# A fused attention and expert kernel: later weight splits and routing in the first slot, memory pools split in two, five accumulator banks instead of three

## The chip, the core and the metric

The kernel runs on one core of a Trainium2 chip. The metric is the device time of one execution in microseconds. The core has a matrix engine (TensorE, PE), a vector engine (VectorE, DVE), a scalar engine (ScalarE, ACT), a general engine (GpSimd, POOL) and a queue for transfers (SyncE, SP). Each works through its own list of instructions strictly in order; they meet at semaphores. Matmul results go to an accumulator memory (PSUM) of eight banks.

## What is computed

Eight batches of 448 tokens, twelve heads of 64. Attention uses a sigmoid instead of a softmax; its output rows (3584 tokens of 768 numbers) go through a mixture of eight experts, of which each token visits the one with the largest logit:

```python
scores = scale * np.matmul(q, k.transpose(0, 1, 3, 2)) - np.log(S)
attn = 1.0 / (1.0 + np.exp(-scores))
x = np.matmul(attn, v)                      # then (B*S, H*D)
logits = x @ w_gate
e_idx = np.argmax(logits, axis=1)           # one expert a token
for e in range(E):
    mask = e_idx == e
    h = np.maximum(x[mask] @ w1[e], 0.0)
    ye = h @ w2[e]
    out[mask] = gate_w[mask, None] * eom[mask, e, None] * ye
```

## The kernel before

**Attention.** 168 units, each of four score matmuls, a sigmoid on ScalarE and four value matmuls. VectorE adds the two halves of an output, transposes it into `xt` (two buffers, one a batch), and at the end of a batch SyncE stores `xt` to `x_dram`. Every two groups the gate matmuls run; after a batch its *routing* follows, a generator with five pieces (`route`): the logits (TensorE transposes, VectorE reductions), the counts (sigmoids, eight small matmuls), the *places* (ScalarE copies the counts out of PSUM, L257; VectorE takes a reciprocal, L258; some fifteen small GpSimd instructions from L259 to L222 make each token's place in the list of its expert), the *rows* (VectorE's reciprocal L271 of what GpSimd made in L267, GpSimd's L273, then four indirect writes into the list `lst` in DRAM, L275, each waiting for the one ahead).

**Slots.** The experts work in slots of 256 rows of one expert. A slot has layer 1 (eight blocks `f` of 18 matmuls, 6 parts of the 768 inputs by 3 products) and layer 2 (four outputs `i` of 24 matmuls). Numbers are kept as a high part, rounded to the matmul's format, and a low part, the rest; high by high, high by low and low by high are summed. So every operand is *split* in two steps (`split`, L421 and L422): ScalarE casts to the high part, VectorE subtracts to get the low part. For a block, ScalarE's relu (L465) writes the high part of `h` and VectorE (L466) the low part; the block's bank is free after that. Three slots (0 to 2) take rows of the first six batches, and can start before the lists are complete; slots 3 to 13 and two half slots at the end follow in the profiled execution.

**What a slot does for the next one.** In `slot`, SyncE loads the next w1 and, later, w2 (each only where the expert changes), GpSimd gathers the next rows from `x_dram` (L399, eight indirect transfers), VectorE transposes them behind block 7 (`turn_x`, L440), and between the outputs of layer 2 the rows and the three pairs of w1 rows are split. The w2 of the slot itself is split during its layer 1, one quarter (`split_w2(k)`, two of the eight inner parts) behind blocks 0, 2, 4 and 6. ScalarE writes each output `y` out of PSUM (L481), and after two of them GpSimd scatters 128 rows to `out` (L483).

**The order around the change.** Nothing reorders: `manual_schedule` keeps the order in which the code is written. The last batch's routing and the tables and lists of the late slots run beside the first slots as a generator `side()`, of which `slot` takes one step after each of blocks 0 to 6 and after outputs 1, 2 and 3, ten steps a slot. Its pieces are: logits at step 2, counts at step 5, places at step 6, rows at step 7; the late table (`table(True)`, five steps on VectorE, L294 to L363) from step 9; then for five groups of lists SyncE's loads (`load_list`) and, three steps later, a VectorE transpose and twelve GpSimd copies (`spread_lists`, L383 to L390).

**Memory and banks.** The attention's buffers form one pool, freed as a whole; the pool of the slots (`late`: `h`, `y`, `w2h`, `w2l` and others) takes its place, so its first writer waits for every reader of the attention's buffers, the store of the last `xt` among them. `take` hands out PSUM banks in turn from a list: layer 1 takes from `psh`, banks 0, 1, 2, 4, 5, of which `build` keeps the first three once attention is recorded (`self.psh = self.psh[0:3]`); layer 2 takes from `psy`, banks 4, 5, 3. A bank is written again only when its last reader is done. Block 0 of slot 0 is already computed inside the attention (`begun`).

Of the kernel before, what the change touches and what calls it, by code (L numbers as in the profile page):

```python
# [9 lines left out]
F32 = mybir.dt.float32  # L10
F32R = mybir.dt.float32r
# [9 lines left out]
B, H, S, D = 8, 12, 448, 64  # L21
NPAIR = H // 2
E = 8
DM = H * D
# [27 lines left out]
class Kernel:  # L52
# [45 lines left out]
        self.tmp_early = o + 4096  # L98

    def late_memory(self):  # L100
        p = self.pool("late")
        self.hs = [p.tile([128, 8, TS], F32R, name=f"h{i}") for i in range(2)]
        self.ys = [p.tile([128, DM], F32, name=f"y{i}") for i in range(2)]
        hb = p.tile([128, DF], F32, name="hb")
        self.hb = hb
        self.hx = p.tile([128, 4, Q4], F32, name="hx")
        self.w2h = p.tile([128, 8, DM], F32R, name="w2h")
        self.w2l = [p.tile([128, 4, DM], F32R, name=f"w2l{i}") for i in range(2)]
        self.lr = [hb[0:32, 192 * i:192 * i + 192] for i in range(5)]

    def tmp(self, shape, dt=F32):
# [375 lines left out]
    def slot(self, cur, nxt, side=None, begun=False, drain=False):  # L487
        nx = self.load_slot(*nxt) if nxt is not None else None
        if drain:
            self.nc.gpsimd.drain()  # L490
        for f in range(8):
            self.layer1(f, begun and f == 0)
            if f % 2 == 0:
                self.split_w2(f // 2)
            if side is not None and f < 7:
                next(side, None)
        self.load_w2(nx)
        self.turn_x(nx)
        self.split_x(nx, 0)
        self.split_x(nx, 1)  # L500
        for i, (t, n) in enumerate(((0, 0), (0, 1), (1, 0), (1, 1))):
            self.layer2(cur, t, n, self.ys[t])
            if i == 0:
                self.split_x(nx, 2)
            if i < 3 and nx is not None:
                self.split_w1(i)
            if side is not None and i > 0:
                next(side, None)
        return nx
# [57 lines left out]
        if nx is not None:  # L567
            self.split_w1_row(5)

    def attention(self, pool):  # L570
        nc = self.nc
        N = B * NPAIR
        NG = N // G
# [1 line left out]
        t = lambda n, shape: pool.tile(shape, F32, name=n)  # L575
# [4 lines left out]
        at = [t(f"a{i}", [128, 2, S]) for i in range(4)]  # L580
        xts = [t(f"x{i}", [128, S]) for i in range(4)]
        xh = t("xh", [128, S])
        xt = [t(f"xt{i}", [128, S // 32, NPAIR * 32]) for i in range(2)]
        half = [slice(0, 64), slice(64, 128)]
        corners = [(0, 0), (1, 0), (0, 1), (1, 1)]

# [78 lines left out]
        for u in range(U * NG + LAG):  # L665
            g, i = divmod(u, U)
# [52 lines left out]
    def build(self, phases="abc"):  # L719
        tc, nc = self.tc, self.nc  # L720
        ms = tc.manual_schedule()
        ms.__enter__()
        self.constants()
        self.memory()
        with tc.tile_pool(name="attn", bufs=1) as p:
            rt = self.attention(p)
        self.late_memory()
        if phases == "ab":
            for _ in rt:
                pass  # L730
            ms.__exit__(None, None, None)
            return

        early = lambda k: (self.tab_e, k, self.lts[:, k], self.lxs[:, k], ROWS_E)
        late = lambda k: (self.tab_l, k, self.lts[:, EARLY + k], self.lxs[:, EARLY + k])

        def side():
            yield
            next(rt)
            yield  # L740
            yield
            yield
            next(rt)
            yield
            for _ in rt:
                yield
            yield
            for _ in self.table(True):
                yield
            nc.gpsimd.memset(self.lr[3], 0.0)  # L750
            groups = [(a, min(a + 4, LATE_N)) for a in range(0, LATE_N, 4)]

            def load(i):
                if i < len(groups):
                    a, b = groups[i]
                    for k in range(a, b):
                        self.load_list(self.tab_l, k, self.lr[i][8 * (k - a):8 * (k - a) + 8], 8)
                else:
                    for k in range(E):
                        self.load_list(self.tab_b, k, self.lr[i][4 * k:4 * k + 4], 4)  # L760

            def spread(i):
                if i < len(groups):
                    a, b = (EARLY + k for k in groups[i])
                    self.spread_lists(self.lr[i], self.lts[:, a:b], self.lxs[:, a:b])
                else:
                    self.spread_lists(self.lr[i], self.ltb, self.lxb)

            for i in range(len(groups) + 1):
                load(i)  # L770
                for _ in range(3):
                    yield
                spread(i)

        self.psh = self.psh[0:3]
        sd = side()
        self.mm_ps = self.mm_late
        cur = self.s0
        for k in range(EARLY - 1):
            cur = self.slot(cur, early(k + 1), sd, k == 0)  # L780
        cur = self.slot(cur, late(0), sd)
        for k in range(LATE_MIN):
            if k == LATE_MIN - 1:
                full = nc.values_load(self.tot[0:1, 0:1], min_val=0, max_val=LATE_MAX)
                part = nc.values_load(self.tot[0:1, 1:2], min_val=0, max_val=E)
                self.gather(dict(lx=self.lxb[:, 1], xg=self.half_x(1)))
            cur = self.slot(cur, late(k + 1), sd, drain=k == LATE_MIN - 1)
        ms.__exit__(None, None, None)
        with ExitStack() as ctx:
            for k in range(LATE_MIN, LATE_MAX):  # L790
                ctx.enter_context(tc.If(full > k))
                with tc.manual_schedule():
                    cur = self.slot(cur, late(k + 1))
        with ExitStack() as ctx:
            for k in range(E):
                ctx.enter_context(tc.If(part > k))
                with tc.manual_schedule():
                    self.half_slot(k, self.ys[k % 2])
# [37 lines left out]
```

## Time and profile before

| | |
|---|---|
| median of 3 runs | 816.55 us (816.5 to 816.66) |
| profiled execution | 817.26 us |
| its span, first to last instruction | 815.5 us |
| TensorE busy | 796.9 us (98%) |
| VectorE, ScalarE, GpSimd busy | 473.5, 459.4, 284.2 us |
| mean granted TensorE clock | 0.994 |

Attention takes the first 283 us of the span, slot 0 until 326.5, slots 1 to 13 until about 770, and the two half slots the rest. Slot numbers follow from layer 2's first matmul (L478): slot 0 at 303.55, slot 1 at 344.21, slot 2 at 378.13, and then every 33.9 us with two exceptions. A row of the timeline has the start, the duration, the engine, the line, the operation, what it writes and reads, and in brackets how long the engine was idle before and what ended that. In a row of windows, `x` counts instructions begun in the window, and the number after the busy time is the granted clock.

### The profile page before, as it was taken

The page shows a single profiled execution, that of the slowest core. Times are in us where ns is not written, and L with a number is a line of the kernel's source. Part 1 is how long each engine was busy: PE and PEld are TensorE (multiplying, and loading weights), DVE is VectorE, ACT ScalarE, POOL GpSimd, SP SyncE. Part 2 cuts the span into 40 slices and gives each one's busy share as a digit, 9 for nine tenths or more (in the row PEclk, how much of TensorE's full clock was granted, in tenths as well). Part 3 has the DMA queues.
Part 4 walks back from the last instruction along what each step waited for, and adds up shares of the span by engine and source line. Part 5 has one row for each costly group of instructions (what it writes and reads, how often), then busy time and mean ns, then how long its engine had stood idle before and what let it go on. Part 6 is the DMA issues. An engine that isn't in the chain of part 4 may idle for free. (4 is left out here: it accounts for less than half of the span.)

```text
span 815.5 us, 16615 instructions
## 1 busy us (share of the span) xinstructions
PE 796.9 (98%) x6540; PEld 621.7 (76%) x6540; DVE 473.5 (58%) x635; ACT 459.4 (56%) x553; POOL 284.2 (35%) x454
## 2 busy tenths in 40 slices
PE   9999999999999998999999999999999999999996
PEld 4333343333333488999999999999999999999985
DVE  2354445445457664865665665656655666565687
ACT  5666666666668544454554555545554555454585
POOL 3003302210234466646524235142353513414142
PEclk9999999999999998999999999999999999999999
DMA  6353443525558220237128661282184211758381
GB/s 249 130 205 133 179 175 127 205 103 174 200 195 331 99 98 20 70 135 259 58 84 285 209 209 65 78 282 87 31 263 144 68 42 38 256 172 302 96 329 39
DMA packets 32316, 126.90 MB, mean 156 GB/s; under 512 B 5535, under 2 KB 7823, under 8 KB 28256
## 3 DMA queue, kind: packets, MB, share of 16 engines
q1 hardware_dynamic: 22288, 100.81, 35.5%
q0 software_dynamic: 9936, 24.88, 9.0%
q8 instruction: 56, 0.92, 0.5%
q14 instruction: 36, 0.29, 0.1%
HBM read 153.15 MB, written 23.64 MB: 217 GB/s over the span
## 5 line engine op out<-in xcount | busy, mean ns | idle before, releaser
L600 ACT ACTIVATE a<-ps,bias_s 128x896 f32<-128x896 f32 x168 | 169.0, 1008 | 99.4 <-PE ps L598 99.4
L455 PE MATMUL ps<-rounded 128*128 128x256 f32 x672 | 191.2, 284 | 1.1 <-DVE h L466 0.9
L457 PE MATMUL ps<-rounded 128*128 128x256 f32 x672 | 190.6, 284 | 1.3 <-DVE rounded L422 1.3
L456 PE MATMUL ps<-rounded 128*128 128x256 f32 x672 | 190.4, 283 | 0.0
L422 DVE TENSOR_TENSOR rounded<-plain,rounded 128x2048 fp32r<-128x2048 f32 (+3 forms) x107 | 149.1, 1413 | 70.9 <-ACT rounded L421 70.8
L480 PE MATMUL ps<-w2h,h 128*128 128x384 f32 x480 | 162.3, 338 | 3.6 <-DVE h L466 3.3
L479 PE MATMUL ps<-w2l,h 128*128 128x384 f32 x480 | 161.9, 337 | 0.6 <-DVE w2l L422 0.6
L478 PE MATMUL ps<-w2h,h 128*128 128x384 f32 x480 | 162.0, 337 | 0.0
L598 PE MATMUL ps<-kqv 64*64 64x448 f32 x1344 | 158.1, 541 | 0.4 <-ACT a L600 0.4
L421 ACT CAST rounded<-plain 128x2048 fp32r<-128x2048 f32 (+3 forms) x107 | 124.7, 1198 | 59.3 <-DVE plain L440 59.3
L607 PE MATMUL ps<-a,kqv 64*64 64x448 f32 x1344 | 157.1, 537 | 0.0
L399 POOL DMA_INDIRECT plain<-x_dram,lxs x120 | 140.2, 1169 | 37.9 <-issue 34.9
L422 DVE TENSOR_TENSOR w2l<-plain,w2h 128x1536 fp32r<-128x1536 f32 x62 | 108.6, 1757 | 49.5 <-ACT w2h L421 49.4
L455 PEld LDWEIGHTS ps<-rounded 128*128 128x128 f32 x672 | 129.0, 192 | 3.1 <-DVE h L466 1.7
L457 PEld LDWEIGHTS ps<-rounded 128*128 128x128 f32 x672 | 129.0, 192 | 1.6 <-DVE rounded L422 1.5
L456 PEld LDWEIGHTS ps<-rounded 128*128 128x128 f32 x672 | 129.0, 192 | 0.0
L483 POOL DMA_INDIRECT out<-y,lts x28 | 36.6, 1307 | 229.6 <-ACT y L481 196.9
L465 ACT ACTIVATE h<-ps 128x256 fp32r<-128x256 f32 x112 | 43.0, 384 | 126.4 <-PE ps L457 117.6
L607 PEld LDWEIGHTS ps<-a,kqv 64*64 64x64 f32 x1344 | 51.8, 133 | 75.3 <-issue 73.9
L598 PEld LDWEIGHTS ps<-kqv 64*64 64x64 f32 x1344 | 48.8, 133 | 74.0 <-issue 62.1
L480 PEld LDWEIGHTS ps<-w2h,h 128*128 128x128 f32 x480 | 91.1, 190 | 4.9 <-DVE h L466 3.6
L479 PEld LDWEIGHTS ps<-w2l,h 128*128 128x128 f32 x480 | 91.1, 190 | 1.0 <-DVE w2l L422 0.9
(179 smaller groups left out, 657.9 us busy)
## 6 DMA issues: line engine op xcount, KB each, us to landing
plain<-w SPq DMA_DIRECT2D x68, 768.0 KB
plain<-w SPq DMA_DIRECT2D x48, 1024.0 KB
kqv<-kqv SPq DMA_DIRECT2D x23, 1344.0 KB
x_dram<-xt SPq DMA_DIRECT2D x8, 1344.0 KB
plain<-w SPq DMA_DIRECT2D x6, 512.0 KB
plain<-x_dram,lxs POOLq DMA_INDIRECT x120, 3.6
kqv<-kqv SPq DMA_DIRECT2D x1, 896.0 KB
lst<-plain POOLq DMA_DIRECT2D x1, 726.0 KB
```

The lines of the kernel that those rows point to most:

```text
L399: self.nc.gpsimd.indirect_dma_start(out=s["xg"][:, g], out_offset=None, in_=x4, in_offset=bass.IndirectOffsetOnAxis(ap=s["lx"][:, g:g + 1] ...
L421: self.nc.scalar.copy(hi, raw)
L422: self.nc.vector.tensor_tensor(lo, raw, r32(hi), ALU.subtract)
L455: nc.tensor.matmul(ps, wh[d][:, c], xh[:, d], start=(d == 0), stop=False)
L456: nc.tensor.matmul(ps, wh[d][:, c], xl[:, d], start=False, stop=False)
L457: nc.tensor.matmul(ps, wl[d][:, c], xh[:, d], start=False, stop=(d == 5))
L478: nc.tensor.matmul(ps, hh[:, f, tk], wh, start=(f == 0), stop=False)
L479: nc.tensor.matmul(ps, hh[:, f, tk], wl, start=False, stop=False)
L480: nc.tensor.matmul(ps, hl[:, f, tk], wh, start=False, stop=(f == 7))
L598: nc.tensor.matmul(ps[half[h], j, 0:S], kg[half[j], e, 0, o:o + 64], kg[half[j], e, 1], start=True, stop=True)
L600: nc.scalar.activation(at[u % 4], ps[:, :, 0:S], AF.Sigmoid, bias=self.bias_s, scale=1.0 / math.sqrt(D))
L607: nc.tensor.matmul(self.ps_o[e][h][half[j], 0:S], v[half[h], 6 if i == 3 else 3 * e + c, j], a[half[h], j], start=(i in ((0, 3 if h else 4 ...
```

## The change

Four edits, all in how the first expert slot joins the attention:

1. In slot 0 (`begun`) the w2 splits stand behind blocks 3, 5 and 7, and the last one behind the third with no block between. Other slots keep 0, 2, 4, 6.
2. `xt` moves to a pool of its own (`attn_x`), and so does `w2l` (`late_w`). By their sizes the pool `late` then lies where the attention's other buffers were, and `w2l` where `xt` was.
3. In `side()` the places move from step 6 to step 8 and the rows from step 7 to step 9, that is from layer 1 of slot 0 to its layer 2; the late table starts at step 10 instead of 9, and the list groups follow one step later each.
4. `psh` keeps its five banks.

```diff
     def late_memory(self):
-        p = self.pool("late")
+        p, q = self.pool("late"), self.pool("late_w")
...
-        self.w2l = [p.tile([128, 4, DM], F32R, name=f"w2l{i}") for i in range(2)]
+        self.w2l = [q.tile([128, 4, DM], F32R, name=f"w2l{i}") for i in range(2)]
...
         for f in range(8):
             self.layer1(f, begun and f == 0)
-            if f % 2 == 0:
+            if begun and f % 2 and f > 1:
+                self.split_w2(f // 2 - 1)
+            elif not begun and f % 2 == 0:
                 self.split_w2(f // 2)
             if side is not None and f < 7:
                 next(side, None)
+        if begun:
+            self.split_w2(3)
         self.load_w2(nx)
...
-    def attention(self, pool):
+    def attention(self, pool, rows):
...
-        xt = [t(f"xt{i}", [128, S // 32, NPAIR * 32]) for i in range(2)]
+        xt = [rows.tile([128, S // 32, NPAIR * 32], F32, name=f"xt{i}") for i in range(2)]
...
-        with tc.tile_pool(name="attn", bufs=1) as p:
-            rt = self.attention(p)
+        with tc.tile_pool(name="attn", bufs=1) as p, tc.tile_pool(name="attn_x", bufs=1) as q:
+            rt = self.attention(p, q)
...
             yield
             next(rt)
             yield
+            yield
+            yield
             for _ in rt:
                 yield
-            yield
             for _ in self.table(True):
                 yield
...
-        self.psh = self.psh[0:3]
         sd = side()
```

What moves shows in three places. The first is VectorE around the end of slot 0's layer 1 and its layer 2 (`L466` is the low half of a block, `L422` a subtraction, on `w2l` or on w1 and rows in `rounded`, `L440` the transpose of slot 1's rows, `L294` the late table's first instruction). Before:

```order
L422 TENSOR_TENSOR w2l_2518<-plain,w2h 128x1536
L466 SCALAR_TENSOR_TENSOR h_2511<-ps,h_2510 128x256
L258 RECIPROCAL sg<-sg 112x32
L466 SCALAR_TENSOR_TENSOR h_2511<-ps,h_2510 128x256
L422 TENSOR_TENSOR w2l_2518<-plain,w2h 128x1536
L271 RECIPROCAL den<-den 112x4
L466 SCALAR_TENSOR_TENSOR h_2511<-ps,h_2510 128x256
L440 STREAM_TRANSPOSE plain<-plain 128x8x6x32
L422 TENSOR_TENSOR rounded<-plain,rounded 128x512 x3
L422 TENSOR_TENSOR rounded<-plain,rounded 128x2048 x3
L294 COPY hb<-last_e 1x1
```

and now:

```order
L466 SCALAR_TENSOR_TENSOR h_2518<-ps,h_2517 128x256 x2
L422 TENSOR_TENSOR w2l_2525<-plain,w2h 128x1536 x2
L440 STREAM_TRANSPOSE plain<-plain 128x8x6x32
L422 TENSOR_TENSOR rounded<-plain,rounded 128x512 x3
L422 TENSOR_TENSOR rounded<-plain,rounded 128x2048 x2
L258 RECIPROCAL sg<-sg 112x32
L422 TENSOR_TENSOR rounded<-plain,rounded 128x2048
L271 RECIPROCAL den<-den 112x4
L294 COPY hb<-last_e 1x1
```

Block 7's low half no longer stands behind L271; the two last `w2l` halves stand behind block 7, and both reciprocals stand among and behind the w1 halves.

The second is GpSimd, from the eight gathers of slot 1's rows on (rows of the places between L261 and L222 are in the same order in both). Before, and now:

```order
L399 DMA plain<-x_dram,lxs 128x192 x8
L259 TENSOR_TENSOR pos<-pc,off 112x32
L261 TENSOR_TENSOR pos<-pos,oh 112x32
L220 TENSOR_TENSOR t_128<-pos 112x16
L221 TENSOR_TENSOR t_129<-t_128 112x8
```

```order
L399 DMA plain<-x_dram,lxs 128x192 x8
L483 DMA out<-y_2519,lts 3584x768
L259 TENSOR_TENSOR pos<-pc,off 112x32
L261 TENSOR_TENSOR pos<-pos,oh 112x32
L220 TENSOR_TENSOR t_128<-pos 112x16
L221 TENSOR_TENSOR t_129<-t_128 112x8
```

The scatter of slot 0's first 128 rows now stands ahead of the places. Behind the places stand, as before, L273, the four list writes L275, a scatter (the second half's alone now) and the eight gathers of slot 2's rows.

The third is TensorE where slot 4's layer 2 begins, with the semaphores that each row waits for. Before:

```order
L457 MATMUL ps<-rounded 128x256
L478 MATMUL ps<-w2h,h_2510 128x384 [waits Activation_49]
L479 MATMUL ps<-w2l_2517,h_2510 128x384
L480 MATMUL ps<-w2h,h_2511 128x384
L478 MATMUL ps<-w2h,h_2510 128x384 [waits Activation_49]
```

and now:

```order
L457 MATMUL ps<-rounded 128x256
L478 MATMUL ps<-w2h,h_2517 128x384 [waits DVE_49]
L479 MATMUL ps<-w2l_2524,h_2517 128x384
L480 MATMUL ps<-w2h,h_2518 128x384
L478 MATMUL ps<-w2h,h_2517 128x384 [waits Activation_49]
```

The first matmul of the output waits for VectorE, which it did not before, and the waits for VectorE that stood further down in this output are gone.

## The prediction

> **What bounds the kernel now.** First the busy shares, then TensorE's waits, then the granted clock around the longest of them.
>
> ```profile
> PE 796.9 (98%) x6540; PEld 621.7 (76%) x6540; DVE 473.5 (58%) x635; ACT 459.4 (56%) x553; POOL 284.2 (35%) x454
> ...
> PE ps L480 <- DVE h L466: 3.3, 1, 3.3
> PE ps L455 <- DVE h L466: 0.9, 2, 0.6
> ...
> 307.71:310.98 3.27, 0.00 (x1) 0.88 0.10 30
> 310.98:316.91 5.93, 5.93 (x19) 0.50 0.02 1
> ```
>
> TensorE sets the time, so an edit counts only where TensorE stops or where its clock drops. The one large stop is in slot 0: 3.27 us, and then 5.93 us at a granted clock of 0.50, which loses half of that, 2.97. The timeline shows the cause:
>
> ```profile
> 288.77 0.36 PE L455 MATMUL ps<-rounded 128*128 128x256 f32 x1
> 290.59 0.38 ACT L465 ACTIVATE h<-ps 128x256 fp32r<-128x256 f32 x1 [8.74 <-DMA x_dram<-xt]
> 303.55 0.34 PE L478 MATMUL ps<-w2h,h 128*128 128x384 f32 x1
> 308.17 0.20 POOL L221 TENSOR_TENSOR t<-t 112x8 f32<-112x8 f32 x1
> 310.20 0.20 POOL L267 TENSOR_TENSOR den<-den,eps 112x4 f32<-112x4 f32 x1
> 310.43 0.18 DVE L271 RECIPROCAL den<-den 112x4 f32<-112x4 f32 x1 [5.31 <-POOL den L267]
> 310.53 0.39 DVE L466 SCALAR_TENSOR_TENSOR h<-ps,h 128x256 fp32r<-128x256 f32 x1
> 326.50 0.28 PE L455 MATMUL ps<-rounded 128*128 128x256 f32 x1
> ```
>
> VectorE stands in its queue at the reciprocal L271, whose input GpSimd makes only after eight gathers; block 7's low half (L466) is queued behind it. At 290.59 the first relu had waited for the store of the rows, which with three banks gave the two waits at L455.
>
> An undisturbed slot gives the yardstick (layer 2 begins, the next slot begins, its layer 2 begins):
>
> ```profile
> 446.79 0.34 PE L478 MATMUL ps<-w2h,h 128*128 128x384 f32 x1
> 463.44 0.28 PE L455 MATMUL ps<-rounded 128*128 128x256 f32 x1
> 480.70 0.34 PE L478 MATMUL ps<-w2h,h 128*128 128x384 f32 x1
> ```
>
> Layer 2 takes 16.65, layer 1 17.26 (2.16 a block), a slot 33.91.
>
> **The change, part by part.** All durations are from the profiled execution: 817.26 us with a span of 815.5; the median of the runs, 816.55, is 1.05 above that span, and I add differences to the median.
>
> *Layer 1 of slot 0.* From 288.77 six blocks and the eight counting matmuls (0.2) need 13.2 and took 14.8. With five banks no block waits, and the pools let the first relu start before 290.59. Layer 2 begins at about 301.95: 1.6 won. Even if the relu still started at 290.59, block 5, the first to take a used bank, starts near 295.4, so the pool split alone is worth nothing beside the banks.
>
> *Weight splits.* The last two now follow block 7.
>
> ```profile
> 301.87 1.46 ACT L421 CAST w2h<-plain 128x1536 fp32r<-128x1536 f32 x1
> 303.37 1.76 DVE L422 TENSOR_TENSOR w2l<-plain,w2h 128x1536 fp32r<-128x1536 f32 x1 [0.94 <-ACT w2h L421]
> ```
>
> ScalarE's relu of block 7 starts at 302.15, its casts at 302.4 and 303.8; VectorE's halves follow 1.5 after the first cast and end near 305.7 and 307.4. TensorE wants the first of them after 13 of layer 2's 96 matmuls, at 304.2, and waits 1.5; the second costs 0.7. Layer 2 lasts 16.65 + 2.2 = 18.85 where it lasted 22.95, and ends at 320.8 instead of 326.50: 5.7 won so far.
>
> *The routing step.* GpSimd's work for places now stands behind the scatter of the first half of slot 0's rows, and L271 behind the last split of w1. What is late next is GpSimd's queue: four list writes, a scatter, and the eight gathers of slot 2's rows.
>
> ```profile
> 311.52 0.20 POOL L273 TENSOR_TENSOR meta<-eom,den 112x4 f32<-112x4 f32 x1
> 312.28 1.00 POOL L275 DMA_INDIRECT lst<-meta,posi  x1 [0.55 <-POOL meta L273]
> 321.10 2.79 POOL L275 DMA_INDIRECT lst<-meta,posi  x1 [1.40 <-DMA lst<-meta,posi]
> 328.03 0.99 POOL L483 DMA_INDIRECT out<-y,lts  x1 [2.83 <-ACT y L481]
> 329.32 0.98 POOL L399 DMA_INDIRECT plain<-x_dram,lxs  x1 [0.30 <-DVE hb L311]
> 340.74 1.83 POOL L399 DMA_INDIRECT plain<-x_dram,lxs  x1 [0.30 <-issue]
> 344.21 0.34 PE L478 MATMUL ps<-w2h,h 128*128 128x384 f32 x1
> ...
> plain<-x_dram,lxs POOLq DMA_INDIRECT x120, 3.6
> ```
>
> Before, the last gather was issued 3.5 ahead of slot 1's layer 2. Now the start of that work is set by VectorE. Slot 1's gathers, which the change does not touch, are issued until about 306, and their rows land 3.6 later, near 309.5. From the transpose of the rows to the last w1 half is a fixed chain through ScalarE and VectorE, 12.7 long in slot 9 (shown below: 623.48 to the matmul at 636.23), so that half ends at 322.2. A GpSimd instruction beside VectorE's long subtraction lasts as long as it:
>
> ```profile
> 380.19 1.97 POOL L387 CAST lxs<-lt 32x24 int32<-32x24 f32 x1 [0.61 <-DVE lt L383]
> 380.36 1.73 DVE L422 TENSOR_TENSOR w2l<-plain,w2h 128x1536 fp32r<-128x1536 f32 x1
> ```
>
> The w1 halves follow each other closely, so most of the places work gets through only from 322.2 on. From L221 to the end of L267 it took 2.2, and 1.1 more to L273: L271 runs at 324.5, L273 at 325.6. VectorE waits 2.3 at L271 again; behind it stand the late table and the low half of slot 1's block 0. TensorE asks for that half only when block 5 wants its bank, 11 us into layer 1, so this wait itself costs nothing: that much of the edit works.
>
> The gathers are another matter. From L273 to the last gather took 29.2 before; less 2.8 of waiting for y and 1.3 for a scatter that now stands ahead, 25.1. I take 21.7, because the four list writes took 11.6 while the long w1 subtractions ran beside them (the write at 321.10 lasted 2.79, the first 1.00), and now run beside the shorter ones of layer 1. Last issue 325.6 + 21.7 = 347.3, landing 350.9, say 351. Ends: 354.4 (25.1 as it stood), 346.8 (GpSimd not held, L273 at 322.6, and 20.6 behind it).
>
> What a late landing costs, the trace shows itself, in slot 9:
>
> ```profile
> 616.36 0.34 PE L478 MATMUL ps<-w2h,h 128*128 128x384 f32 x1
> 623.48 1.78 DVE L440 STREAM_TRANSPOSE plain<-plain 128x1536 f32<-128x1536 f32 x1 [5.15 <-DMA plain<-x_dram,lxs]
> 636.23 0.39 PE L457 MATMUL ps<-rounded 128*128 128x256 f32 x1 [1.31 <-DVE rounded L422]
> 651.92 0.34 PE L478 MATMUL ps<-w2h,h 128*128 128x384 f32 x1
> ```
>
> Here four more gathers stand ahead and the rows came late: the transpose began 7.1 after layer 2, and the next layer 2 came 28.4 after the transpose, paced by the chain. A transpose up to 5.5 after layer 2 is free (33.91 − 28.4). Slot 1's layer 2 begins at 320.8 + 0.9 (first bank wait below) + 17.26 = 338.95; 351.0 is 12 behind it. Slot 2's layer 2 then begins at 351.0 + 28.4 + 0.5 (a list transpose that the later routing puts between the last two halves) = 379.9:
>
> ```profile
> 378.13 0.34 PE L478 MATMUL ps<-w2h,h 128*128 128x384 f32 x1
> ```
>
> It was 378.13: everything won in slots 0 and 1 is waited away, and 1.8 more. (Inside slot 1 the table also delays block 6's low half, in whose bank the first output lies, to about 341; the rows are later still, so it adds nothing.) The loads of lists that SyncE issues move by one step too, in the same order; their users now come later than the lists, so they cost nothing. In slot 2 the list transposes stand one block later and wait for GpSimd's copies behind the gathers; with five banks layer 1 runs on, and layer 2 meets the last two w2 halves some 0.3 later than before (an estimate from L422's 1.73 and the 2.1 us that twelve such copies take). Ends of this term: 375.7 and 383.3, that is −2.4 and +5.2.
>
> *Five banks.* Layer 1 used banks 0, 1, 2 for the rest of the kernel, and layer 2 4, 5, 3; now layer 1 takes 0, 1, 2, 4, 5 in turn. With 8 blocks and 4 outputs a slot, the banks follow from counting. In slots 4 and 12 layer 2's first output takes the bank of block 7 (5 and 4), and waits for its low half, which VectorE makes behind the last w2 half. Slots 1 and 8 and the second half slot open in the bank of the output before, and wait for ScalarE's copy.
>
> ```profile
> 448.35 0.42 DVE L466 SCALAR_TENSOR_TENSOR h<-ps,h 128x256 fp32r<-128x256 f32 x1
> 719.75 0.34 PE L478 MATMUL ps<-w2h,h 128*128 128x384 f32 x1
> 721.30 0.42 DVE L466 SCALAR_TENSOR_TENSOR h<-ps,h 128x256 fp32r<-128x256 f32 x1
> 565.17 0.28 PE L455 MATMUL ps<-rounded 128*128 128x256 f32 x1
> 565.43 0.58 ACT L481 ACTIVATE y<-ps,lts 128x384 f32<-128x384 f32 x1 [1.79 <-PE ps L480]
> 789.60 0.39 PE L543 MATMUL ps<-rounded 128*128 128x512 f32 x1
> 789.80 0.58 ACT L481 ACTIVATE y<-ps,ltb 128x384 f32<-128x384 f32 x1 [1.03 <-PE ps L480]
> ```
>
> Each costs from TensorE's start to the reader's end: 448.77 − 446.79 = 2.0 and 721.72 − 719.75 = 2.0, plus about 0.05 each; 566.01 − 565.17 = 0.9; 790.38 − 789.60 = 0.8. Nothing behind them gives it back: 5.8. Slot 1's 0.9 is inside the gathers' term.
>
> **Sum.** +1.8 + 0.3 + 5.8 = +7.9: span 823.4, median 824.4.
>
> **Rivals.** *A, the rows are not late:* GpSimd overtakes what I hold it for and the transpose is in time. For it: GpSimd is only 35% busy. Against: all its queue is serial. Then slot 2's layer 2 begins at 338.95 + 33.91 = 372.9, and −5.2 + 0.3 + 5.8 = +0.9: 817.4. *B, the bank waits vanish,* if something else is late there anyway: +2.1, 818.7. Against: slots 4 and 12 show no other wait. *C, faster: both.* −5.2 + 0.3: 811.6; it decides if the rows land before 338.95 + 5.5 = 344.5. *D, the clock also drops* after one of the new waits. The 3.27-us wait did it, the 1.31-us one did not; mine are 2.0, and, near 361, two waits in 4 us with 0.7 of work between. One drop costs 2.97: 827.4.
>
> [...]
>
> **How the numbers follow.** Forecast 0.58, A 0.13, B 0.11, C 0.05, D 0.13. Predicted: 824.4. The range 817.5 to 829 takes in the landing's ends (−2.4 and +5.2 with the other 6.1: 820.2 and 827.9), B and D, and has A at its edge. Half of A and a third of B fall within 0.2% (1.6 us, about what a measurement of this kernel can tell from no change): faster 0.06, same 0.13, slower 0.81.
>
> **What would show it.** Right: the 3.27-us stop and the 0.50 clock gone from slot 0 and slot 1 beginning near 321.7; waits of TensorE for L422 of w2l in slot 0's layer 2; a wait of VectorE's L440 of some 8 us in slot 1; new TensorE waits of about 2 us at L478 in two slots. Wrong: slot 2's layer 2 before 375, or slots 4 and 12 still 33.9 long. Slot 0 still stopping for L271 would mean that the step is not late enough.

## The result, and the profile after

The changed kernel takes 835.17 us (median of 4 runs, 833.83 to 835.97) beside 816.61 for the kernel before on the same chip (816.5 to 817.23): a ratio of 1.0237, with a 95% interval of 1.0215 to 1.0258. It is slower, by 18.6 us where 7.9 were forecast. The profiled execution has a span of 833.7, the granted clock of TensorE is 0.991 on average.

TensorE still sets the time. The first line of the page, and then the table of TensorE's waits in the profile after (what waited, for whom: us in total, times, the longest):

```profile
PE 801.5 (96%) x6540; PEld 623.5 (75%) x6540; DVE 473.9 (57%) x635; ACT 460.1 (55%) x553; POOL 285.1 (34%) x454
...
PE ps L479 <- DVE w2l L422: 5.0, 4, 2.3
PE ps L457 <- DVE rounded L422: 4.6, 4, 1.6
PE ps L478 <- DVE h L466: 3.7, 2, 1.9
PE ps L547 <- ACTq L793: 2.8, 1, 2.8
PE ps L478 <- ACT hb L556: 0.7, 1, 0.7
PE ps L547 <- ACT y L481: 0.7, 1, 0.7
```

The stop of 3.3 at L480 is gone, as wanted. In its place stand many waits of 0.7 to 2.8 us. They fall into places that the timeline gives (line numbers beyond some 495 are four higher than before). TensorE's rows at the waits, after:

```profile
305.36 0.44 PE L479 MATMUL ps<-w2l,h 128*128 128x384 f32 x1 [1.35 <-DVE w2l L422]
321.34 0.39 PE L455 MATMUL ps<-rounded 128*128 128x256 f32 x1 [0.67 <-ACT y L481]
382.84 0.44 PE L479 MATMUL ps<-w2l,h 128*128 128x384 f32 x1 [2.28 <-DVE w2l L422]
385.17 0.69 PE L479 MATMUL ps<-w2l,h 128*128 128x384 f32 x1 [1.01 <-DVE w2l L422]
387.39 0.69 PE L480 MATMUL ps<-w2h,h 128*128 128x384 f32 x1 [0.57 <-DVE h L466]
455.08 0.44 PE L478 MATMUL ps<-w2h,h 128*128 128x384 f32 x1 [1.87 <-DVE h L466]
733.30 0.44 PE L478 MATMUL ps<-w2h,h 128*128 128x384 f32 x1 [1.87 <-DVE h L466]
786.91 0.63 PE L547 MATMUL ps<-rounded 128*128 128x512 f32 x1 [2.78 <-ACTq L793]
816.99 0.44 PE L478 MATMUL ps<-w2h,h 128*128 128x384 f32 x1 [0.75 <-ACT hb L556]
```

The first two are slot 0 and the start of slot 1, 5.2 earlier than before (326.50). The next three are in layer 2 of slot 2, then come slots 4 and 12, and the start and the second layer 2 of the half slots. Behind some of these waits the granted clock is down (windows of TensorE: length, busy time, its instructions, granted clock, DMA share, GB/s):

```profile
385.00:388.00 3.00, 2.26 (x6) 0.50 0.87 294
388.00:391.00 3.00, 3.00 (x11) 0.50 1.03 414
455.00:458.00 3.00, 2.92 (x11) 0.67 0.76 210
733.00:736.00 3.00, 2.69 (x15) 1.00 0.67 178
787.00:790.00 3.00, 3.00 (x8) 0.52 0.80 194
```

From the first matmuls of each layer the program falls into five stretches. The table gives their lengths in us; the fifth ends where the first half slot starts, so it holds the wait ahead of it, and the last one ends where the last layer 2 starts. An undisturbed slot is 33.9.

| kernel | slot 0 | slot 1 and layer 1 of slot 2 | layer 2 of slot 2 | slots 3, 4 | slots 5 to 13 | half slots |
|---|---|---|---|---|---|---|
| before | 43.6 | 51.6 | 17.5 | 67.8 | 308.2 | 26.9 |
| after | 39.0 | 56.8 | 23.7 | 71.6 | 313.5 | 30.1 |
| difference | −4.6 | +5.2 | +6.3 | +3.7 | +5.3 | +3.2 |

In three of the four sets of runs below the kernel before itself took 823 to 824 us, its variants' slot 0 beginning at 287 to 289 instead of 282.5; those sets are compared by the ratio to the kernel before of the same set, and by the lengths of stretches. Of the kernel before there is one profile only, the one of this table.

### The profile page after: what moved, and what is told of

It reads as the page before. It is cut to its first block, busy times and chain, and to the rows that moved or that the text cites. A ratio compares the mean times of both kernels' runs of the same rounds, so it can differ in the third digit from the quotient of the medians.

```text
span 833.7 us, 16605 instructions
## 1 busy us (share of the span) xinstructions
PE 801.5 (96%) x6540; PEld 623.5 (75%) x6540; DVE 473.9 (57%) x635; ACT 460.1 (55%) x553; POOL 285.1 (34%) x454
## 5 line engine op out<-in xcount | busy, mean ns | idle before, releaser
L422 DVE TENSOR_TENSOR rounded<-plain,rounded 128x2048 fp32r<-128x2048 f32 (+3 forms) x107 | 149.1, 1413 | 72.7 <-ACT rounded L421 72.4
L480 PE MATMUL ps<-w2h,h 128*128 128x384 f32 x480 | 162.6, 339 | 0.6 <-DVE h L466 0.6
L422 DVE TENSOR_TENSOR w2l<-plain,w2h 128x1536 fp32r<-128x1536 f32 x62 | 108.5, 1757 | 51.4 <-ACT w2h L421 49.4
L465 ACT ACTIVATE h<-ps 128x256 fp32r<-128x256 f32 x112 | 43.1, 385 | 130.1 <-PE ps L457 125.3
```

Of the source, the lines that this page charges most:

```text
L422: self.nc.vector.tensor_tensor(lo, raw, r32(hi), ALU.subtract)
L480: nc.tensor.matmul(ps, hl[:, f, tk], wh, start=False, stop=(f == 7))
```

## Experiments

### Each edit undone, or alone

These four ran together; the kernel before took 816.26 beside them.

**Five banks alone.** The kernel before with one line taken out:

```diff
-        self.psh = self.psh[0:3]
```

> The kernel before with the fourth edit alone: five banks for layer 1 (the truncation to three taken out). Theory: from slot 3 on the whole loss comes from the banks, waits and clock drops behind them, and needs nothing of the other edits: about +12 of the +18, so 828, with waits of about 2.0 us at L478 in slots 4 and 12, a granted clock near 0.7 behind the one in slot 4, and a wait of some 2.8 us at the first half slot. Rival: only the counted waits are the banks' (+5.8), the clock drops and the half slot's wait come from the later routing: 822. Second rival: five banks pay for themselves in slot 0 (-1.6) and the sum is 820.

Measured: 826.17 us, ratio 1.012 (1.0075 to 1.0164). Stretches: 44.8, 51.3, 17.5, 71.6, 311.4, 28.5. Slot 3 begins at 396.25, 0.6 later than before; from there on it shows the changed kernel's +3.7 in slots 3 and 4 and its waits in slots 8 and 12. So the waits and the clock drop of slot 4 are the banks' own work. One point of the expectation missed: the half slots begin as in the kernel before, after a wait of 1.0 and with no clock lost (28.5 is the 26.9 of before with the banks' 0.9 and 0.7). That part of the loss is not the banks'. Layer 1 of slot 0 takes 19.9 here, where it took 20.6 before and takes 19.2 in the changed kernel: five banks win only half of what was won there, since the first relu still starts at 290.34 and a counting matmul waits 0.56 for VectorE.

**Three banks in the changed kernel.** The same line put back ahead of the slots.

```diff
         cur = self.s0
+        self.psh = self.psh[0:3]
         for k in range(EARLY - 1):
```

> The changed kernel with three banks again for layer 1 from slot 0's second block on. Theory: the +12 from slot 3 on go, the +6.3 up to slot 3 stay, because the late rows and the late list transposes of slot 2 do not depend on banks: 823. Rival: five banks are also what lets layer 2 of slot 2 run into its missing low halves and drop the clock; with three banks layer 1 is held instead, the clock stays at 1.00 and slot 3 begins 3 us earlier: 820.

Measured: 824.97 us, ratio 1.0109 (1.0066 to 1.0153). Stretches: 38.1, 63.3, 17.2, 67.8, 309.7, 29.7. So 10.2 us go, where 12 were expected. Slots 3 and 4 are undisturbed, and slots 5 to 13 lose 3.8 less. The start of slot 3 hardly moved (401.43 instead of 401.88): what layer 2 of slot 2 no longer loses, its layer 1 loses now. TensorE's row in slot 2, and the windows behind it:

```profile
380.18 0.58 PE L455 MATMUL ps<-rounded 128*128 128x256 f32 x1 [3.79 <-DVE h L466]
...
379.00:382.00 3.00, 1.82 (x8) 0.50 0.02 5
382.00:385.00 3.00, 3.00 (x15) 0.50 0.27 49
```

With three banks layer 1 waits for VectorE's low half of block 4, in whose bank block 7 must go; with five it runs on, and layer 2 meets the late low parts of w2. Both stand behind the same VectorE instruction, the list transpose L383 of the section on lists below, and both lose clock behind it. The theory holds, and the rival, that five banks let the clock drop, falls.

**The routing steps of before.** In the changed kernel, the order of `side()` as before.

```diff
             next(rt)
             yield
-            yield
-            yield
             for _ in rt:
                 yield
+            yield
```

> The changed kernel with the routing steps of before (counts, places and rows behind blocks 4, 5 and 6 of slot 0, the late table one step earlier). Theory: the gathers of slot 2 and the list transposes are in time again, slot 2 loses nothing and slot 3 begins near 413 instead of 419.1: 835.2 - 6 = 829; slot 0 has its stop at L480 back (near 3 us) but that is waited away in slot 1. Rival: slot 2's stall comes from the five banks and stays: 833 to 836.

Measured: 829.23 us, ratio 1.0164 (1.0121 to 1.0207). Stretches: 44.5, 51.3, 17.5, 71.6, 313.2, 30.3; slot 3 begins at 395.90. All of the +6.3 up to slot 3 is gone, as expected, although slot 0 has a stop of 5.74 us again, and half clock behind it (0.50 from 310 to 313). So in the changed kernel the later routing takes away the 5.5 us that slot 0 wins by it, and 6 more.

**The splits of before.** Behind blocks 0, 2, 4, 6 in slot 0 too.

```diff
-            if begun and f % 2 and f > 1:
-                self.split_w2(f // 2 - 1)
-            elif not begun and f % 2 == 0:
+            if f % 2 == 0:
                 self.split_w2(f // 2)
...
-        if begun:
-            self.split_w2(3)
```

> The changed kernel with the splits of w2 in slot 0 behind blocks 0, 2, 4, 6 again. Theory: slot 0's layer 2 loses its waits for w2l (1.35 and 0.34 us), slot 1 begins about 1.7 earlier, and this is waited away at slot 1's w1 halves, because GpSimd sets the start of the gathers: 835. Rival: the gathers follow slot 0, and the 1.7 stay: 833.5.

Measured: 829.21 us, ratio 1.0165 (1.0119 to 1.0211). Stretches: 36.7, 61.1, 19.5, 71.5, 310.7, 28.5. Both expectations missed. Slot 0 is 2.3 shorter, and slot 1 begins at 319.25. Slot 3 begins 1.9 earlier: of the 2.1 at slot 1 little was waited away. What changed in between is where the clock dropped: here it dropped behind two waits for w1 of 1.32 and 1.63 us in layer 1 of slot 2 (0.50 from 363 to 366), and in layer 2 it stayed at 1.00. Of the profile's other 4.5 us, 0.8 is in slot 10, and 3.6 is at the half slots, which begin after a wait of 0.83 instead of 2.78, and at full clock (1.00 from 782.1 to 785), as with five banks alone. An edit in slot 0 changed something 500 us later.

### The branch ahead of the half slots

Between slot 13 and the half slots stand the branches that skip the slots that this input does not need. TensorE waits there for ScalarE's own branch (`ACTq L793` is ScalarE's sequencer at the `If`). ScalarE has the same work in all kernels, but not the same number of synchronising instructions: the late splits save seven of them. So in the built programs every branch lies seven places earlier in ScalarE's program in the kernels with the late splits, while the distance to its target is the same in all. In the three kernels so far without the late splits (the kernel before, five banks alone, the splits of before) TensorE waited 0.83 to 1.18 us, in the three with them 2.71 to 3.00. To separate the place from the edit, seven instructions of no use were put at the very start of the changed kernel:

```diff
-        nc.scalar.activation(self.warm_t(cp), self.bias_s, AF.Sigmoid)
+        w = self.warm_t(cp)
+        for _ in range(8):
+            nc.scalar.activation(w, self.bias_s, AF.Sigmoid)
```

> The changed kernel with seven more one-column activations on ScalarE at the very start, while it waits for its first data. Nothing else moves but the place of ScalarE's later instructions in its program: the branch ahead of the half slots becomes its instruction 796, as in the kernel before and in the two runs where that branch was quick, instead of 789. Theory: how long ScalarE takes over that branch hangs on where the branch and its target lie in its instruction stream; the wait of 2.78 us falls to about 1.1 and the clock stays up behind it, so 835.2 - 3.2 = 832. Rival: the wait comes from the work ahead of the branch (the late scatter, the weights' splits), and the time stays at 835.

Measured: ratio 1.0266 (1.023 to 1.0303), and in a second set:

> The changed kernel with the seven added activations at the start of ScalarE's program, once more. Theory: 3.2 less than the changed kernel, a ratio of 1.020 beside 1.024; the wait ahead of the half slots 1.1 instead of 2.78. Rival: no difference in the whole time.

Measured: ratio 1.0286 (1.0245 to 1.0328). TensorE's row at the start of the half slots and the window behind it, in the second:

```profile
795.44 0.47 PE L549 MATMUL ps<-rounded 128*128 128x512 f32 x1 [0.88 <-ACTq L795]
...
795.40:798.40 3.00, 2.96 (x13) 1.00 0.59 134
```

The wait is 0.88 instead of 2.78, and the clock 1.00 instead of 0.52; the half slots take 28.4 instead of 30.1. The wait is 0.8 to 1.2 in eleven profiles with the branch at its place of before, and 2.7 to 3.0 in the six with it seven earlier. That the place in the program decides is shown, and it costs 1.6 to 1.9 at the wait, and 1.7 of clock behind it. (The 796 and 789 that the expectation gives belong to the first `If`, ahead of slot 10, which ScalarE meets at 644.3 us in the changed kernel and whose block is used here. The branch of this wait is the fifth, 173 instructions behind it in every program. So the numbers were another branch's, and the shift by seven is the same.) In the whole time the 3.2 cannot be seen: single runs of these two kernels lie up to 3.6 us off their medians, and the ratios stand between the 1.0237 of the changed kernel and the 1.0292 of its control in a later set (below). The ratio of 1.020 that was expected did not come, and the rival, no difference in the whole time, is not refuted.

What makes the one place slow and the other quick, no trace shows.

### The single tile for transposed lists

In layer 1 of slot 2, VectorE stood at a list transpose (L383). VectorE's rows in the changed kernel, with what is queued behind the transpose, and then GpSimd's:

```profile
371.05 0.42 DVE L466 SCALAR_TENSOR_TENSOR h<-ps,h 128x256 fp32r<-128x256 f32 x1
380.31 0.51 DVE L383 STREAM_TRANSPOSE lt<-hb 32x192 f32<-32x192 f32 x1 [8.83 <-DMA hb<-lst]
380.75 0.37 DVE L466 SCALAR_TENSOR_TENSOR h<-ps,h 128x256 fp32r<-128x256 f32 x1
381.05 1.73 DVE L422 TENSOR_TENSOR w2l<-plain,w2h 128x1536 fp32r<-128x1536 f32 x1
382.71 0.74 DVE L466 SCALAR_TENSOR_TENSOR h<-ps,h 128x256 fp32r<-128x256 f32 x2
383.38 1.73 DVE L422 TENSOR_TENSOR w2l<-plain,w2h 128x1536 fp32r<-128x1536 f32 x1
386.52 0.50 DVE L383 STREAM_TRANSPOSE lt<-hb 32x192 f32<-32x192 f32 x1 [1.41 <-POOL lts L390]
...
366.33 1.64 POOL L399 DMA_INDIRECT plain<-x_dram,lxs  x1 [0.30 <-issue]
377.26 0.95 POOL L399 DMA_INDIRECT plain<-x_dram,lxs  x1 [0.30 <-issue]
378.25 0.20 POOL L387 CAST lxs<-lt 32x32 int32<-32x32 f32 x1
380.08 0.19 POOL L390 COPY lts<-lt 32x8 f32<-32x8 f32 x1
```

The transpose writes `lt`, of which there is one. GpSimd copies the list before out of it only behind the eight gathers of the next slot, and is done at 380.27; VectorE goes on at 380.31. (The profile names a transfer, but the loads of this list had landed by 371.3.) With the routing of before (rows of the run with the routing undone) the same collision ends at nearly the same time, but falls one list later, at a point where only one quarter of w2 is left to make:

```profile
379.86 0.53 DVE L383 STREAM_TRANSPOSE lt<-hb 32x192 f32<-32x192 f32 x1 [3.84 <-POOL lts L390]
380.33 0.37 DVE L466 SCALAR_TENSOR_TENSOR h<-ps,h 128x256 fp32r<-128x256 f32 x1
380.63 1.74 DVE L422 TENSOR_TENSOR w2l<-plain,w2h 128x1536 fp32r<-128x1536 f32 x1
```

A second tile for late lists takes the wait away without taking away its cause, the copies' place:

```diff
-        t = self.lt32
+        spare = self.gl[0][0:32, 0:192].rearrange("p (w t) -> p w t", t=32)
+        t = self.take("t", [self.lt32, spare]) if lt.shape[1] > 2 else self.lt32
```

> The changed kernel with a second tile for the transposed lists in layer 2's time, so that VectorE's list transpose no longer waits until GpSimd has copied the list before out of the only one. Theory: in slot 2 VectorE no longer stands at L383 until 380.3; the last halves of w2 are there in time, TensorE's waits of 2.28, 1.01 and 0.57 and the 3 us at half clock behind them go: 6 to 7 less, 829, slot 3 from about 395.5. Rival: VectorE is late there because the rows were late (its whole chain from L440 on), and the list only comes last: 1 to 2 less, 834.

Measured: ratio 1.0225 (1.0187 to 1.0264), beside 1.0266 for the padded kernel of the same set. And once more:

> The changed kernel with the second list tile, once more. Theory: layer 2 of slot 2 at 16.7 instead of 23.7; slot 1's layer 2 to slot 3's layer 1 takes 57 instead of 63: 835 - 6 = 829, a ratio of 1.016. Rival: part of it comes back as a clock drop behind the two waits for w1 in layer 1 of slot 2: 832, 1.020.

Measured: ratio 1.0185 (1.0145 to 1.0226), beside 1.0286 for the padded one. VectorE's rows in the first (its lines are one higher):

```profile
376.31 0.52 DVE L384 STREAM_TRANSPOSE gl<-hb 32x192 f32<-32x192 f32 x1
381.58 0.52 DVE L384 STREAM_TRANSPOSE lt<-hb 32x192 f32<-32x192 f32 x1
391.35 0.51 DVE L384 STREAM_TRANSPOSE gl<-hb 32x192 f32<-32x192 f32 x1 [0.22 <-DMA hb<-lst]
```

In the first run no transpose waits for GpSimd; in the second only the last one does, for 1.41 us. Layer 2 of slot 2 takes 16.7 and 17.9. By themselves these two lengths prove little, since layer 2 began late there (at 388.3 and 386.3, when the padded kernels' stalls were over, at 385.4); the pair of runs that differs in the tile alone stands in the last section of these experiments. The changed kernel once more, as a control in a later set, has 24.3 there:

> The changed kernel once more, as the control for the others of this call: 835, ratio 1.023; in slot 2's layer 2 the waits for w2l and h (some 3.9 us) and a granted clock near 0.5 behind them. If the drop is a matter of the moment, the waits are there again and the drop is not: then 832.

Measured: ratio 1.0292 (1.0253 to 1.0331), above the 1.023 expected. In slot 2 the waits (2.28, 1.02, 0.89) and the drop to 0.50 came again. Both changes together:

> The changed kernel with the second list tile and the seven added activations of pad_act together; the two act in different places and are read apart by slots. Theory: layer 2 of slot 2 falls from 23.7 to 16.7, and the branch ahead of the half slots costs 3.2 less: 835 - 7 - 3.2 = 825. Rival for the first: layer 1 of slot 2 or slot 3 takes over what layer 2 no longer waits, and only 3.2 go: 832.

Measured: ratio 1.0212 (1.0163 to 1.0262), 0.8% below the control of the same set, some 6.6 us where 10 were expected. In the profiles, slot 1 and slot 2 up to slot 3 together take 80.6 in the control, 78.1 and 77.9 in the two padded kernels, which kept the single tile but had no such drop in layer 2 (1.00 there), and 75.1, 74.2 and 79.5 in the three runs with the second tile. In the last of these (an execution of 849.4 us, the median was 843.9) layer 2 took 16.65, but layer 1 of slot 2 took 26.8: TensorE stopped there four times, for 2.4 us in all, where the profile names no one (`issue`), and its clock was down to 0.53 from 385 to 390. So by these profiles the tile is worth 3 to 6 us twice, and about 1 or nothing the third time. In the whole times the three runs are 0.4, 1.0 and 0.8% below the kernel with the single tile in their sets, and the last two of these differences lie clear of noise. The theory is right on what goes in layer 2; its size is not settled, and the rival of the last run, that layer 1 takes over what layer 2 no longer waits, is what that run's profile shows. The kernel before takes 69.1 here; most of the rest is the late rows of slot 2.

### The later routing alone

> The kernel before with the third edit alone: the two last routing steps and the late table later, with three banks, the splits of before and no pools of their own. Theory: slot 0 loses its stop at L480, slot 1 begins near 321; the rows of slot 2 are issued and land later, and the list transposes of slot 2 hold VectorE; slot 3's layer 2 comes near 418 (before: 412.88), and nothing else differs: +5.5, a ratio of 1.007. Rival: the late routing costs this only together with five banks, which let layer 2 of slot 2 begin before its halves are ready; with three the gain of slot 0 stays: -3, 0.996.

The kernel before with the third edit alone. Measured: 830.24 us, ratio 1.0085 (1.0052 to 1.0118). Stretches: 37.3, 64.0, 16.7, 68.5, 310.9, 26.9. The stop in slot 0 is gone (layer 2 there takes 16.65), and 6 us are won by slot 1; slot 1 and layer 1 of slot 2 give back 12.4. It needs neither banks, pools nor splits. The rival falls. By the medians this part costs about 7 us, less than the five banks alone (10). Three stops of TensorE's in layer 1 of slot 2, 2.6 us together, for which the profile names no one, and a lower clock behind them (0.59 from 386 to 389) are in the 12.4, so the price in stretches, 5.3 up to slot 3, is uncertain by about as much.

### Pools alone, and a routing step that is later by one block

**Pools.** The kernel before with the second edit alone.

> The kernel before with the second edit alone (the rows of the last batch and the low halves of w2 in pools of their own). Theory, from the run with three banks, whose layer 1 of slot 0 was as short as with five: the pools alone bring layer 1 of slot 0 from 20.65 to about 19.2; the stop at L480 behind GpSimd's routing work grows by the same, and the time stays: 816.5. Rival, as predicted: layer 1 stays at 20.65 with three banks, and nothing moves at all. Second rival: 815, if the stop does not grow.

Measured: 821.05 us, ratio 0.9961 (0.9938 to 0.9985): a gain of 0.4%, the only one of the three edits tried alone that gains; the stop at L480 stayed at 3.3 us, so the second rival is the one that came. Layer 1 of slot 0 takes 19.42 with three banks; it took 20.65 in the kernel with the third edit alone, in a like set, and 19.19 in the changed kernel both with five banks and with three. The first relu (L465) of slot 0 shows why, before (quoted with the prediction: 290.59, behind the store of the rows), after, and with three banks again:

```profile
285.85 0.38 ACT L465 ACTIVATE h<-ps 128x256 fp32r<-128x256 f32 x1 [4.53 <-PE ps L642]
...
286.23 0.39 ACT L465 ACTIVATE h<-ps 128x256 fp32r<-128x256 f32 x1 [4.53 <-PE ps L642]
```

**The last routing step behind block 7.** What the change wanted, VectorE's low half of block 7 ahead of the reciprocal L271, needs only one block's delay, not a move into layer 2. With the pools:

```diff
-            if side is not None and f < 7:
+            if side is not None and f < 8 and f != (6 if begun else 7):
                 next(side, None)
```

> The kernel before with the pools, and the last routing step (L271 on VectorE, the four list writes on GpSimd) issued behind block 7 of slot 0 instead of behind block 6, so that the low half of block 7 and the last split of w2 stand ahead of the reciprocal that waits for GpSimd. Three banks, splits and the other routing steps as before. Theory: TensorE no longer stops 3.3 us at L480 nor runs 5.9 us at half clock; some 4 of the 6 lost in slot 0 come back, the rest is waited away at slot 1's w1 halves; the gathers of slot 2 are not later than before: 812. Rival: what slot 0 wins is waited away in slots 1 and 2, since GpSimd and the gathers' landing set them: 816.

Measured: ratio 0.9983 (0.9952 to 1.0015): the rival came. And in a second set:

> The kernel of rows_last once more, on the chip of the other runs of this call. Theory: it keeps its stall at L383 in slot 2 and stands within 0.3% of the kernel before; the difference to rows_lists is 3 to 4 us. Rival: no difference between the two, since the list tile was not what held VectorE.

Measured: ratio 0.996 (0.9938 to 0.9982), 820.96 us. Slot 0's layer 2 takes 16.65 in both, and slot 1's layer 2 begins 2.7 earlier than with the pools alone, counted from the start of slot 0; then in slot 2 the list tile takes that back, layer 2 there lasting 20.3 and 20.5, with waits of 5.10 and 4.31 us of VectorE's at L383. Together with the second tile:

> The kernel before with the pools, the last routing step behind block 7 of slot 0, and a second tile for the transposed lists. Theory: in slot 2 of the run without the second tile VectorE stood 5.1 us at L383 for GpSimd's copies, and layer 2 lost 3.7 there; with the second tile that goes, and the 3.5 to 5 us won in slots 0 and 1 stay: 812 beside 816.5 for the kernel before, a ratio of 0.994 to 0.995. Rival: layer 1 of slot 2 meets late w1 halves instead (the rows land at 349 as before), and the time is that of the kernel before.

Measured: ratio 0.9947 (0.9926 to 0.9967), 820.08 beside 823.46. Layer 2 of slot 2 begins at 379.15, beside 378.41 without the second tile, and takes 17.15 instead of 20.54: the one pair of one set that differs in the tile alone, and it shows what the stall at L383 costs there, 3.4 us. In the whole time the two lie only 0.9 us apart, where 3 to 4 were expected. And again, on another chip:

> The kernel before with the pools, the last routing step behind block 7 and the second list tile, once more. Theory: 3.5 to 5 us below the kernel before, a ratio of 0.994 to 0.995. Rival: the gain was a matter of the session with late transfers, and the ratio is 0.998 to 1.000.

Measured: 0.9953 (0.9929 to 0.9978), 818.67 beside 822.9. So this kernel stands 3.4 and 4.2 us below the kernel before. The pools alone had given 3.3 of that (0.9961, in another set); up to slot 3 this kernel is 3.6 to 3.9 us shorter than with the pools alone, but in the whole time that is not shown. Stretches of the second: 36.1, 54.4, 17.1, 68.5, 312.0, 26.9. Slot 0 is shorter here than with the change (39.0); some 3 us of that are waited away in slot 1 for w1 and for the bank of a low half:

```profile
327.97 0.39 PE L458 MATMUL ps<-rounded 128*128 128x256 f32 x1 [1.30 <-DVE rounded L423]
335.76 0.39 PE L456 MATMUL ps<-rounded 128*128 128x256 f32 x1 [0.57 <-DVE h L467]
```

## Why the prediction was wrong

The direction was right, the size was not: 824.4 was forecast, 835.17 came, and the range ended at 829. The terms one by one:

- *Layer 1 of slot 0: right in size, wrong in reason.* 1.6 was forecast, 1.5 came. But it is the pools that bring it: with three banks in the changed kernel it is the same 19.19. The prediction held that the pool split alone is worth nothing beside the banks; it is the wrong way round, since the relu starts at 285.85 instead of 290.59, and then no block waits for a bank. Five banks alone gave 0.7 of the 1.5.
- *Splits: right.* TensorE waits 1.35 and 0.34 for w2l (forecast 1.5 and 0.7), and slot 1 begins at 321.34 (forecast 320.8 and a bank wait of 0.9).
- *Routing: right, two misses in part cancelling.* GpSimd's L273 ran at 323.35 (forecast 325.6), but from there to the last gather it took 23.1 (forecast 21.7); slot 2's rows reached VectorE's L440 at 349.37 (forecast 351), and slot 2's layer 2 began at 378.14 (forecast 379.9; it was 378.13 before). All that slots 0 and 1 had won was waited away. The runs with the routing undone and alone confirm it.
- *The list transposes: the step that failed.* It put layer 2 "some 0.3 later". The stall was named rightly, but its size was taken from durations, without asking when it ends and what stands behind it. It ends when GpSimd has issued eight gathers and made twelve copies, at 380.27, though layer 2 begins at 378.14; behind it on VectorE stand the low halves of blocks 4 to 7 and the last two of the four w2 splits. TensorE waited 2.28 + 1.01 + 0.57 = 3.86, and the clock then halved for 6 us, 3 us more. Layer 2 of slot 2 took 23.74 instead of 17.48: 6.3 instead of 0.3. That the stall makes TensorE wait is shown by the pair of runs with and without the second tile (3.4 us there); that the later routing puts it one list earlier, with more work queued behind, by the run with the routing undone.
- *Banks: right to a tenth where they were counted.* The waits at slots 4 and 12 are 1.87 (layers 2.0 longer each), at slot 8 0.73 and at the second half slot 0.67 (0.9 longer each): 5.8 in all. One wait was missed: in the second half slot layer 2 waits 0.75 for ScalarE's relu of `hb`, again only with five banks; it lost 0.7.
- *Clock drops: a rival that came three times.* D was priced at one drop, 2.97, with a chance of 0.13. Drops came in slot 2 (3.0), in slot 4 (1.7) and at the first half slot (1.6).
- *The branch: in no term and no rival.* 1.6 at the wait, with the 1.6 of clock just named behind it. (The table's +3.2 for the half slots is another sum: that 1.6 of clock, and the 0.9 and 0.7 of the banks.)

The differences of the profiles add up: 0.0 until slot 2's layer 2, then 6.3 (lists) + 5.8 (banks) + 0.7 (`hb`) + 1.7 (clock in slot 4) + 3.2 (branch) + 0.5 (a longer wait for w1 in slot 10) = 18.2, as much as the span is longer. Against the forecast of 7.9 that is 10.3 more: 6.0 from the list transposes, 3.2 from the branch, 1.7 + 0.7 + 0.5 from the three others, less the 1.8 that the routing was to lose and did not. Rivals A, B and C are refuted: the rows are late, and the bank waits stand. The causes by cost, each with a run that takes it away or has it alone: five banks (8 to 8.5 in the stretches from slot 3 on, 10 in the times with and without them), late routing (6 to 7), and the late splits (6 when undone in the changed kernel, 3.6 of it at the branch; alone they were not run); the pools win some 3 back.

What stays open is when a short wait drops the clock, what makes the branch quick or slow, and what TensorE's stops are for which the profile names no one.

## What to carry to other kernels

When a step is moved later on an engine that works strictly in order, follow every later meeting of that engine with the others, not only the wait that is being cured: here the cure of one stop in slot 0 put more of VectorE's work behind another meeting of the two engines in slot 2, at a staging tile that they share. Price a stall by its end time and by what is queued behind it, never by the duration of the work it waits for. And where the goal is only to let one instruction pass another, move it by one place and no further: with the pools, one block's delay and a second staging tile came out 3 to 4 us below the kernel before, nearly all of which the pools give alone, while the larger move lost about 7.

## What the chip showed that was not expected

**Short waits halved the clock, and the same wait did not always.** The prediction had one drop behind a wait of 3.27 and none behind 1.31, and gave little chance to a drop between. In slot 4 of the changed kernel a wait of 1.87 us brought the clock to 0.67 over the next 3 us; the identical wait in slot 12 left it at 1.00. In the control run of the same kernel, TensorE's row and window in slot 12:

```profile
744.28 0.44 PE L478 MATMUL ps<-w2h,h 128*128 128x384 f32 x1 [1.87 <-DVE h L466]
...
744.00:747.00 3.00, 2.72 (x11) 0.68 0.77 240
```

So the same wait at the same instruction dropped the clock in one execution and not in another. Over the ten profiles with five banks, a wait of 1.87 us stood in slot 4 four times, and the clock fell behind each (slots 3 and 4 took 71.5 to 71.6 us, where 67.8 and the wait's 2.0 make 69.8); it stood in slot 12 six times, and the clock fell behind two (the window above, and in the second run with the second tile, where TensorE's matmuls were 0.32 us apart from 737.7 to 740.9 instead of 0.17). In the padded kernel's second run a wait of 2.57 us in slot 4 left it up: the matmuls behind it stayed 0.17 us apart. Two waits of 1.3 and 1.6 us with about 1 us of work between did it in slot 2 with the splits of before (0.50 from 363 to 366), and not in the changed kernel (1.00 from 360 to 370). At the half slots, waits of 0.83 to 1.22 left the matmuls 0.23 us apart eight times out of eight, and those of 2.71 to 2.87 put them 0.43 us apart four times out of four. A wait of about 2 us should be priced here at its length, and some 1.7 us more in many executions (here six of the ten waits of 1.87).

**Seven instructions more or fewer on ScalarE changed the wait at a branch by 1.6 to 1.9 us**, some 500 us after slot 0, as shown above.

**GpSimd copies beside a long VectorE subtraction took ten times as long.** The prediction had seen one such row; here it came twice in a row. In slot 2 of the changed kernel two of the twelve list copies lasted 1.98 and 2.02 us where the others lasted 0.2, each beside a subtraction L422 (at 381.05 and 383.38, shown above); the rows of GpSimd:

```profile
380.88 1.98 POOL L387 CAST lxs<-lt 32x32 int32<-32x32 f32 x1 [0.60 <-DVE lt L383]
383.17 2.02 POOL L387 CAST lxs<-lt 32x32 int32<-32x32 f32 x1
385.50 0.20 POOL L387 CAST lxs<-lt 32x32 int32<-32x32 f32 x1
```
